# Three moves in a written order: a mask table, the second expert's pick, the first expert's rows

## The chip, the cores and the metric

The kernel runs on 1 core of one Trainium2 chip. The core has five engines, each with a queue of its own that it works off in order: TensorE (PE in the profile; its weight loads are PEld), VectorE (DVE), ScalarE (ACT), GpSimd (POOL) and SyncE (SP). SP issues most transfers, POOL and ACT issue some. The metric is device time of one execution in microseconds (us); 475.47 us is the median of three runs of the kernel before.

## The reference

Three layers are computed in float32: windowed attention with a few global positions, a routed expert layer in which a token may keep the expert of the token before it, and a gated two-matrix layer.

```python
scores = scale * q @ k.T - slopes * dist          # B=2, H=8, S=768, D=64; slopes = 2**-(h+1)
keep = (pos[None, :] < 8) | ((rel >= 0) & (rel < 96))
a = softmax(where(keep, scores, -1e9));  x = a @ v            # x: 2 x 768 x 512

logits = x @ w_gate                                # 8 experts
local_gate = sigmoid(x @ w_local)
e[s] = argmax(logits[s]) if s == 0 or local_gate[s] < 0.5 else e[s - 1]
out[s] = softmax(logits[s])[e[s]] * (relu(x[s] @ w1[e[s]]) @ w2[e[s]])   # 512 -> 1024 -> 512

xk = mu_k * x + (1 - mu_k) * x_prev;  xr = mu_r * x + (1 - mu_r) * x_prev
out = sigmoid(xr @ w_r) * (relu(xk @ w_k)**2 @ w_v)
```

## The kernel before

**Attention.** The 2 x 768 tokens are twelve tiles of 128. Each tile takes two steps of the main loop (`i`, 24 in all, `t, g = divmod(i, 2)`), one for each four heads. A step has six parts: scores on TensorE into PSUM (`emit_S`); masks and minima on VectorE (`emit_min`, L922: score plus a mask table `tb`, and the row's minimum); exponentials on ScalarE (`emit_exp`, L934, with row sums); transposes of the weights (`emit_pT`, L941 and L943, into banks PT); their eviction to SBUF, one half by VectorE and one by ScalarE (`emit_ev`, L952 and L950, tiles `pt`); and output products (`emit_pv`, L966, into a bank O), which come one or two steps later. `emit_xT` (L971) evicts the finished tile `xT`, `turn_x` (L188) turns it to rows, and `route_x` (L193) writes rows `X`.

**Mask tables.** The eight tables of 128 x 232 (`tables`, L604) are made by VectorE in the first steps. They wait in a list `tq`; `NTAB` says how many are taken at the end of a step.

**Routing.** It runs in pairs of tiles, spread over the attention's steps: logits on TensorE (`route_lgt`, L215, bank R), maxima and candidates `ab` on VectorE (`route_max`, `route_max2`), `ab` turned into rows (`route_rows`, L267; ScalarE evicts half of it as `br`, L270), a scan over the tokens (`route_scan`, L278, `er`), the one-hot `OH` (`route_oh`, L291), and sums of it on TensorE (`route_sum`, L303 and L307) that give every row its place in the expert's region. GpSimd scatters the rows to HBM (`scatter`, L311).

**First experts early.** The expert with most rows so far is picked from the first tiles (`early_pick` rank 0), and the kernel begins its work before the routing is over. A second pick (rank 3, matmul L375, `bonus` L373, `early_index` cast L380) names the next expert; `values_load` (L983) reads the cast's result on SP. The first expert's first 128 rows are read back from HBM into `xe` (`early_x`, L990), turned and split into a high and a low part: `early_split` transposes (L693), evicts the high part on ScalarE (`exexh`, L695) and subtracts on VectorE (`exexl`, L697). All matmuls of the experts are three products of such parts (`mm3`, L683 to L685, with weights `whi`, L667, and `wlo`, L672). The remaining work of the first expert is fed in by a generator (`fill`, advanced by `F_`) between the last steps of the routing.

**What sets the order.** The order on every engine is the order in which this code is written (`tc.manual_schedule`). In the main loop there are named points (`Rs`, `Ra`, `Dq`, `Dm`, ...): `at(i, point, f)` puts routing work at a point of step `i`, and `do(i, point)` runs it there. The last step (`i = 23`) is written out behind the loop. A tile's PSUM bank is taken from a pool by its tag (S, T, O, PT, R); bank R exists once, so every user of it waits for the reader of the one before.

Of the kernel before, what the change touches and what calls it, by code (L numbers as in the profile page):

```python
# [47 lines left out]
XW = (3, 4, 5, 7)  # L48
NIN = 4
NI = 2 * NTT  # L50
NTAB = (5, 4)
X1_AT = (5, 7)
WNEXT = (1, 1, 1, 0, 0, 1, 2, 1, 2, 1, 2, 0) + (0,) * 4
EARLY_AT = (7, 9, 9, 10, 10, 11, 11, 11, 12, 12, 12, 13, 13, 13, 15, 15, 15, 15)
# [564 lines left out]
def build(ctx, tc, ins, out):  # L619
    n = Net(ctx, tc, ins, out)  # L620
# [352 lines left out]
    def early_split(a):  # L973
        ex = [ap.tile([P, KD, P], F32R, tag=tg, bufs=2, name=f"ex{tg}{a}") for tg in ("exh", "exl")]
        yield from split_steps(xe[a], *ex, 0, n.bank("T", 1) if a else n.bank("S", 2))
        xe[a] = ex
# [4 lines left out]
    def early_start(rank, r):  # L981
        fi = n.early_index(rp, rank)
        wsrc[r] = nc.values_load(fi[:, 0:1], engines=(SP,), min_val=0, max_val=E - 1)  # L983
# [23 lines left out]
    def at(i, point, *fs):  # L1007
        plan.setdefault((i, point), []).extend(fs)
# [12 lines left out]
    for g in groups:  # L1021
        i = 2 * g[-1] + 3
        lgg, mx, mx2, rows, scan, tn, oh, sm_, ps_, acc = (lambda f=f, g=g: f(ap2, g) for f in (
            lambda _, g: n.route_lgt(ap2, g, xTs), n.route_max, n.route_max2, n.route_rows, n.route_scan, n.route_turn, n.route_oh, n.route_sum,
            lambda _, g: pos(g), n.route_acc))
        if g[-1] == NTT - 1:
            tail = mx, mx2, rows, scan, tn, oh, sm_, ps_
            continue
        at(i, "Rb", lgg)
        at(i + 1, "E0" if g[-1] < NTT - 3 else "Ra", lambda g=g: n.route_lge(ap2, g))  # L1030
        at(i + 1, "Rb", lambda g=g: n.route_lgb(ap2, g))
        at(i + 1, "Db", mx)
        if g[-1] < NTT - 3:
            at(i + 1, "Db", mx2)
        if g[-1] == NTT - 3:
            tail8 = mx2, rows, scan, tn, oh, sm_, ps_, acc
            continue
        at(i + 2, "Ra", rows)
        at(i + 2, "Dm", scan)
        at(i + 3, "Rt", tn, oh)  # L1040
        at(i + 3, "Rb", sm_)
        if g[-1] in (5, 7):
            e = g[-1] == 7

            def count(g=g, e=e):
                nm = "cnte" if e else "cnt6"
                setattr(n, nm, n.counted(rp, g, nm))
                n.route_mm(ap2, g)
                n.order_a(ap2, "fg"[e], getattr(n, nm), n.fvec if e else None)

            at(i + 3, "Rb", count)
            at(i + 3, "Db", lambda g=g: pos(g, False), acc)
            at(i + 3, "Rc", n.order_k)
            at(i + 3, "Dc", lambda e=e: n.order_c(ap2, "fg"[e], rp))
            at(i + 4, "Ra" if e else "Rs", lambda e=e: n.early_pick(rp, 3 * e))
            at(i + 4, "Dm" if e else "Dq", lambda e=e: early_start(3 * e, e))
        else:
            at(i + 3, "Db", ps_, acc)

    with tc.manual_schedule():  # L1060
# [99 lines left out]
        for i in range(NI - 1):  # L1160
            t, g = divmod(i, 2)
            late = g == 1 and i > 1
            ahead = [] if i and not g else [u for u in (i + 1, i + 2) if u < NI and u // 2 == (i + 1) // 2]

            def scores():
                for u in ahead:
                    emit_S(u)
                for u in ahead:
                    if u // 2 % NT < NT - 1:
                        emit_kglob(u)  # L1170
                if i == 0:
                    emit_kglob(0)

            def next_kq(*turned):
                emit_kT(t + 1, *turned[0:1])
                if t + 2 < NTT:
                    load("k", t + 2)
                emit_qT(t + 1, *turned[1:2])
                if t + 2 < NTT:
                    load("q", t + 2)  # L1180

            turned = []
            if late:
                scores()
                emit_xT(t - 1)
                emit_exp(i, 0)
                emit_exp(i, 1)
                do(i, "Rs")
                emit_pT(i - 1, 0)
                emit_pT(i - 1, 1)  # L1190
                if i < NI - 2:
                    emit_min(i + 1)
                do(i, "Dq")
                emit_ev(i - 1, 0)
                emit_ev(i - 1, 1, True)
                do(i, "Ra")
                n.turn_x(xTs[t - 1], t - 1, "O" if i < NI - 3 else "S")
                do(i, "Dm")
            else:
                if i > 2 and t + 1 < NTT and not g:  # L1200
                    turned = [turn4(kn.pop(t + 1)), turn4(qn.pop(t + 1))]
                do(i, "Rt")
                if 0 < i:
                    emit_pT(i - 1, 0)
                    emit_pT(i - 1, 1)
                do(i, "Ra")
                emit_exp(i, 0)
                do(i, "E0")
                if turned:
                    next_kq(*turned)  # L1210
                if 0 < i:
                    emit_ev(i - 1, 0)
                    emit_ev(i - 1, 1, True)
                if i == 2:
                    turned = [None]
                    next_kq()
                emit_exp(i, 1)
                if i and g == 0:
                    n.route_ri(t - 1, stat[t - 1][1])
                do(i, "Dm")  # L1220
            bg_early()
            if i == 1:
                n.routing_consts()
            if not late:
                scores()
            if scq:
                scatter(scq.pop(0))
            if g == 0 and t + 1 < NTT and not turned:
                next_kq()
            do(i, "Rb")  # L1230
            bg_early()
            if i < NI - 2 and not late:
                emit_min(i + 1)
            if late:
                if t - 1 in XW[::2]:
                    n.xw = wp.tile([P, 2 * D], F32, tag="whi", bufs=9, name=f"xw{t - 1}")
                n.route_x(ap, X, t - 1)
            do(i, "Db")
            for u in (i - 2, i - 1) if i and not g else ():
                emit_pv(u, 0)  # L1240
                emit_pv(u, 1)
            do(i, "Rc")
            do(i, "Dc")
            if g == 0 and 0 < t and (t + 1) % NT and t + 1 < NTT:
                load_vp(t + 1)
            for _ in scq[:2]:
                scatter(scq.pop(0))
            if g == 1 and t + 2 < NTT:
                load("v", t + 2)
            if 0 < i <= E // 2:  # L1250
                for e in (2 * i - 2, 2 * i - 1):
                    nc.scalar.dma_start(out=n.xs[e * REG:e * REG + PRE, :], in_=n.warm)
            if tq:
                for _ in range(NTAB[i]):
                    if tq:
                        tq.pop(0)()
                if not tq:
                    tstack.close()
                    n.counters(ap)
                    dp = astack.enter_context(tc.tile_pool(name="dp", bufs=1, reuse_waits="tile"))  # L1260
                    dwa = dp.tile([P, 1024], F32, name="dwa")
            if i == 2:
                n.routing_fill()
            if i == 3:
                n.gate_rest()
                n.mix_load()
            if i == 4:
                n.mix_rest()
                n.limits(n.const)
            if 0 in wsrc and early is None:  # L1270
                early = True
                ld_q = list(range(4))
                hi_q = [None] * 3 + [(c, s_) for c in range(NIN) for s_ in range(2)]
                bg_early()
            if i in (4, 11, 17):
                dec_load(PIECES[(4, 11, 17).index(i)], dwa)
            if i in (7, 12):
                dgen = dec(PIECES[i // 12], word_tile)
            if i in (7, 8, 9, 12, 13, 15):
                next(dgen, None)  # L1280
            if i == NI - 2:
                dec_load(PIECES[3], qzz)
# [11 lines left out]
        i = NI - 1  # L1294
# [6 lines left out]
        mx2()  # L1301
        emit_min(i)
        emit_ev(i - 1, 1, True)
        first_rows = early_split(0)
        next(first_rows)
        n.turn_x(xTs[a], a)
        rows()
        scan()
        n.route_x(ap, X, a)
        for _ in first_rows:  # L1310
            pass
        emit_exp(i, 0)
        emit_exp(i, 1)
        for _ in range(2):
            bg_early(0)
        emit_pv(i - 1, 0)
        emit_pv(i - 1, 1)
        tn()
        oh()
        while hi_q or lo_q:  # L1320
# [730 lines left out]
```

## Time and profile before

| | |
|---|---|
| median of 3 runs | 475.47 us (474.75 to 476.24) |
| the profiled execution | 478.9 us, span 477.1 us |
| TensorE busy | 461.9 us (97%) |
| VectorE busy | 345.2 us (72%) |
| ScalarE busy | 267.1 us (56%) |
| GpSimd busy | 115.9 us (24%) |
| read from and written to HBM | 73.49 MB and 12.71 MB |

The span goes from the first instruction to the last; the execution's own time is 1.8 us longer. Attention with the routing fills about the first 106 us, the experts follow, and the last layer closes. All times below count from the span's start. Matmuls are pipelined: a row's duration overlaps that of the next one, so distances between starts tell more than durations.

### The profile page before, as it was taken

The page shows a single profiled execution, that of the slowest core. Times are in us where ns is not written, and L with a number is a line of the kernel's source. Part 1 is how long each engine was busy: PE and PEld are TensorE (multiplying, and loading weights), DVE is VectorE, ACT ScalarE, POOL GpSimd, SP SyncE. Part 2 cuts the span into 40 slices and gives each one's busy share as a digit, 9 for nine tenths or more (in the row PEclk, how much of TensorE's full clock was granted, in tenths as well). Part 3 has the DMA queues.
Part 4 walks back from the last instruction along what each step waited for, and adds up shares of the span by engine and source line. Part 5 has one row for each costly group of instructions (what it writes and reads, how often), then busy time and mean ns, then how long its engine had stood idle before and what let it go on. Part 6 is the DMA issues. An engine that isn't in the chain of part 4 may idle for free. (4 is left out here: it accounts for less than half of the span.)

```text
span 477.1 us, 9261 instructions
## 1 busy us (share of the span) xinstructions
PE 461.9 (97%) x3210; PEld 399.4 (84%) x3210; DVE 345.2 (72%) x911; ACT 267.1 (56%) x657; POOL 115.9 (24%) x204
## 2 busy tenths in 40 slices
PE   7999999989999999999999999999999999999994
PEld 5888888768788889879879887898989898898984
DVE  5878898986859867988897988897848767363301
ACT  3898888974437735577696686752424324152320
POOL 4212212202300000000010013061844819162220
PEclk9999999999999999999999999999999999999999
DMA  7997586967576887799699733004738450200001
GB/s 178 252 225 175 147 212 204 281 208 235 182 246 217 301 288 242 237 332 311 210 357 405 249 117 111 23 2 128 281 100 279 138 185 38 88 1 23 23 3 49
DMA packets 76491, 86.90 MB, mean 182 GB/s; under 512 B 50676, under 2 KB 50932, under 8 KB 76436
## 3 DMA queue, kind: packets, MB, share of 16 engines
q1 hardware_dynamic: 68176, 63.01, 42.2%
q0 software_dynamic: 4944, 17.17, 11.1%
q10 hardware_dynamic: 3316, 6.03, 3.5%
q8 instruction: 28, 0.46, 0.4%
q14 instruction: 27, 0.22, 0.1%
HBM read 73.49 MB, written 12.71 MB: 181 GB/s over the span
## 5 line engine op out<-in xcount | busy, mean ns | idle before, releaser
L667 ACT ACTIVATE whi<-wraw 128x512 fp32r<-128x512 f32 x128 | 72.4, 623 | 6.9 <-ACT yo L786 2.2
L676 DVE TENSOR_TENSOR wlo<-wraw,whi 128x1024 fp32r<-128x1024 f32 x55 | 66.1, 1218 | 2.9 <-ACT whi L667 2.4
L1562 ACT ACTIVATE sq<-S 128x256 f32<-128x256 f32 x48 | 18.5, 385 | 72.9 <-PE S L685 72.5
L683 PE MATMUL S<-xkh,whi 128*128 128x256 f32 x192 | 54.3, 283 | 0.2 <-ACT whi L667 0.2
L685 PE MATMUL S<-xkh,wlo 128*128 128x256 f32 x192 | 53.3, 278 | 0.2 <-DVE wlo L672 0.2
L1572 POOL TENSOR_TENSOR kl<-sq,kh 128x256 fp32r<-128x256 f32 x40 | 36.6, 923 | 69.5 <-issue 36.6
L684 PE MATMUL S<-xkl,whi 128*128 128x256 f32 x192 | 53.2, 277 | 0.0
L1602 DVE TENSOR_TENSOR o<-O,sig 128x512 f32<-128x512 f32 (+1 forms) x13 | 8.4, 650 | 50.9 <-PE O L685 31.7
L684 PE MATMUL O<-wlo,kh 128*128 128x512 f32 (+1 forms) x104 | 39.1, 376 | 0.7 <-DVE wlo L672 0.7
L685 PE MATMUL O<-whi,kl 128*128 128x512 f32 (+1 forms) x104 | 39.1, 376 | 0.0
L683 PE MATMUL O<-whi,kh 128*128 128x512 f32 (+1 forms) x104 | 38.7, 373 | 0.0
L683 PEld LDWEIGHTS S<-xkh,whi 128*128 128x128 f32 x192 | 36.1, 188 | 0.7 <-ACT whi L667 0.4
L685 PEld LDWEIGHTS S<-xkh,wlo 128*128 128x128 f32 x192 | 36.1, 188 | 0.4 <-DVE wlo L672 0.4
L684 PEld LDWEIGHTS S<-xkl,whi 128*128 128x128 f32 x192 | 36.1, 188 | 0.2
L1563 DVE SCALAR_TENSOR_TENSOR sq<-S,sq 128x256 f32<-128x256 f32 x48 | 20.1, 421 | 15.8 <-ACT sq L1562 15.3
L1571 ACT ACTIVATE kh<-sq 128x256 fp32r<-128x256 f32 x48 | 19.7, 412 | 12.9 <-DVE sq L1563 12.9
L684 PEld LDWEIGHTS O<-wlo,kh 128*128 128x128 f32 x104 | 19.5, 188 | 4.9 <-DVE wlo L672 1.1
L683 PEld LDWEIGHTS O<-whi,kh 128*128 128x128 f32 x104 | 19.5, 188 | 3.7
L685 PEld LDWEIGHTS O<-whi,kl 128*128 128x128 f32 x104 | 19.6, 188 | 3.5
L311 POOL DMA_INDIRECT xs<-X,posi x8 | 9.6, 1197 | 44.0 <-DVE acc L333 18.6
L952 DVE COPY pt<-PT 128x512 f32<-128x512 f32 (+1 forms) x24 | 15.4, 641 | 5.9 <-PE PT L943 4.2
L966 PE MATMUL O<-pt,vn 128*64 128x128 f32 x192 | 18.7, 281 | 0.6 <-ACT pt L950 0.4
(488 smaller groups left out, 1424.0 us busy)
## 6 DMA issues: line engine op xcount, KB each, us to landing
wraw<-in_moe_w_dram SPq DMA_DIRECT2D x64, 512.0 KB
dwt<-in_moe_w_v_dram POOLq DMA_DIRECT2D x8, 512.0 KB, 4.2
z<-in_moe_w_k_dram SPq DMA_DIRECT2D x8, 512.0 KB
z<-in_moe_w_v_dram SPq DMA_DIRECT2D x8, 512.0 KB
ys<-yo ACTq DMA_DIRECT2D x13, 256.0 KB
vn<-in_v_dram SPq DMA_DIRECT2D x12, 256.0 KB
xn<-xs SPq DMA_DIRECT2D x12, 256.0 KB
dwt<-in_moe_w_k_dram POOLq DMA_DIRECT2D x6, 512.0 KB, 6.4
```

The lines of the kernel that those rows point to most:

```text
L311: self.nc.gpsimd.indirect_dma_start(self.xviews[t], bass.IndirectOffsetOnAxis(ap=self.posi[:, t:t + 1], axis=0), X[t], None)
L667: nc.scalar.activation(out=whl[r, c][0][:, sl], in_=raws[r, c][:, sl], func=ACTF.Copy)
L676: nc.vector.tensor_tensor(lo, raws.pop((r, c)), hi.bitcast(F32), op=ALU.subtract)
L683: nc.tensor.matmul(out_, lhsT=ah, rhs=bh, start=first, stop=False)
L684: nc.tensor.matmul(out_, lhsT=ah, rhs=bl, start=False, stop=False)
L685: nc.tensor.matmul(out_, lhsT=al, rhs=bh, start=False, stop=last)
L952: nc.vector.tensor_copy(d[:, 0:ps.shape[1]], ps)
L966: nc.tensor.matmul(Os[t][a * HD:(a + 1) * HD, p * P:(p + 1) * P], lhsT=src[:, h * HD:(h + 1) * HD], rhs=d[:, (2 * c + a) * P:(2 * c + a + ...
L1562: nc.scalar.activation(out=sq_, in_=ps[:, 0:TB], func=ACTF.Relu)
L1563: nc.vector.scalar_tensor_tensor(sq_, ps[:, 0:TB], 0.0, sq_, op0=ALU.max, op1=ALU.mult)
L1571: nc.scalar.activation(out=hh, in_=sq_, func=ACTF.Copy)
L1572: (nc.gpsimd if b else nc.vector).tensor_tensor(hl, sq_, hh.bitcast(F32), op=ALU.subtract)
```

## The change

Three pieces of work change their place; no operation is added or taken away. First, the list of mask tables is emptied between the two evictions of step 2, and `NTAB` takes fewer at the end of step 1. Second, the second pick moves to a new point `Rp` ahead of the minima of step 21, and its cast to `Dq`, behind the minima and ahead of the evictions. Third, in the last step its exponentials and the output products of the step before it come ahead of `early_split(0)`, which began right behind the evictions.

```diff
-NTAB = (5, 4)
+NTAB = (5, 2, 0)
...
-            at(i + 4, "Ra" if e else "Rs", lambda e=e: n.early_pick(rp, 3 * e))
-            at(i + 4, "Dm" if e else "Dq", lambda e=e: early_start(3 * e, e))
+            at(i + 4, "Rp" if e else "Rs", lambda e=e: n.early_pick(rp, 3 * e))
+            at(i + 4, "Dq", lambda e=e: early_start(3 * e, e))
...
                 emit_pT(i - 1, 0)
                 emit_pT(i - 1, 1)
+                do(i, "Rp")
                 if i < NI - 2:
                     emit_min(i + 1)
                 do(i, "Dq")
...
                     emit_ev(i - 1, 0)
+                    while i == 2 and tq:
+                        tq.pop(0)()
                     emit_ev(i - 1, 1, True)
...
-            if tq:
+            if tq or i == 2:
                 for _ in range(NTAB[i]):
...
         emit_ev(i - 1, 1, True)
-        first_rows = early_split(0)
-        next(first_rows)
         n.turn_x(xTs[a], a)
         rows()
         scan()
+        emit_exp(i, 0)
+        emit_exp(i, 1)
+        emit_pv(i - 1, 0)
+        emit_pv(i - 1, 1)
+        first_rows = early_split(0)
+        next(first_rows)
         n.route_x(ap, X, a)
         for _ in first_rows:
             pass
-        emit_exp(i, 0)
-        emit_exp(i, 1)
         for _ in range(2):
             bg_early(0)
-        emit_pv(i - 1, 0)
-        emit_pv(i - 1, 1)
         tn()
         oh()
```

On VectorE, at the mask tables, there stood (a `pt` is evicted from bank PT, `tb` is a mask table, `RI` the reciprocal of row sums):

```order
L922 ISA peexl,nm_309<-S_296,tb 128x232
L922 ISA nm_309 128x1
L604 SCALAR_TENSOR_TENSOR tb<-rel,mw 128x232 x3
L952 COPY pt_0_340<-PT_332 128x256
L198 TENSOR_SCALAR RI<-sm_208 128x8
```

and now there stands

```order
L922 ISA peexl,nm_309<-S_296,tb 128x232
L922 ISA nm_309 128x1
L604 SCALAR_TENSOR_TENSOR tb<-rel,mw 128x232 x2
L952 COPY pt_0_329<-PT_321 128x256
L604 SCALAR_TENSOR_TENSOR tb<-rel,mw 128x232
L198 TENSOR_SCALAR RI<-sm_208 128x8
```

One table, the eighth, has gone behind the eviction. On VectorE, at the second pick in step 21, there stood (`Rg` is the ranking, `fi` the index that SP reads, `R` the bank of the pick; four minima stand between the first two rows and the eviction):

```order
L364 TENSOR_SCALAR Rg<-iota_e,rkg 8x8
L922 ISA peexh,nm_1694<-S_1666,tb 128x232
...
L922 ISA peexl,nm_1694<-S_1667,tb 128x232
L922 ISA nm_1694 128x1
L952 COPY pt_0_1700<-PT_1684 128x512
L373 SCALAR_TENSOR_TENSOR bonus<-Rf,Rg 8x1
L380 CAST fi_1713<-R_1706 1x1
L672 TENSOR_TENSOR wlo_1_1605<-wraw_1_1458,whi_1_1604 128x512 x2
```

and now there stands

```order
L364 TENSOR_SCALAR Rg<-iota_e,rkg 8x8
L373 SCALAR_TENSOR_TENSOR bonus<-Rf,Rg 8x1
L922 ISA peexh,nm_1698<-S_1666,tb 128x232
...
L922 ISA peexl,nm_1698<-S_1667,tb 128x232
L922 ISA nm_1698 128x1
L380 CAST fi_1704<-R_1696 1x1
L952 COPY pt_0_1716<-PT_1684 128x512
L672 TENSOR_TENSOR wlo_1_1605<-wraw_1_1458,whi_1_1604 128x512 x2
```

`bonus` has gone ahead of the minima and the cast ahead of the eviction; on TensorE the pick keeps its place. On TensorE, in the last step, there stood (`xe` holds the first expert's rows, `xT` the finished tile, `R` receives the rows of `ab`, `O` the output products):

```order
L943 MATMUL PT_1810<-ident,peexl 128x128
L693 MATMUL S_1831<-ident,xe_1664 128x128 x4
L188 MATMUL PT_1837<-ident,xT_1815 128x128 x4
L267 MATMUL R_1842<-ident,ab_1781 1x128 x4
L966 MATMUL O_1862<-pt_0_1817,vn_1565 64x128 x2
...
L966 MATMUL O_1862<-pt_1_1827,vp 64x128 x2
L286 MATMUL R_1871<-ones_r,er_1849 128x8 x2
```

and now there stands

```order
L943 MATMUL PT_1810<-ident,peexl 128x128
L188 MATMUL PT_1829<-ident,xT_1815 128x128 x4
L267 MATMUL R_1834<-ident,ab_1781 1x128 x4
L966 MATMUL O_1847<-pt_0_1817,vn_1565 64x128 x2
...
L966 MATMUL O_1847<-pt_1_1827,vp 64x128 x2
L693 MATMUL S_1858<-ident,xe_1664 128x128 x4
L286 MATMUL R_1871<-ones_r,er_1841 128x8 x2
```

The four transposes of `xe` have gone behind the output products. On ScalarE, in the same step, there stood (the four rows L934 are the last step's exponentials):

```order
L950 ACTIVATE pt_1_1827<-PT_1810 128x512
L695 ACTIVATE exexh_1829<-S_1831 128x512
L270 ACTIVATE br_1847<-R_1842 1x256
L934 ACTIVATE zbig,sm_1695<-zbig,nm_1694 128x232
...
L934 ACTIVATE peb_108,sm_1695<-peb_108,nm_1694 128x232
L667 ACTIVATE whi_4_1893<-wraw_4_1624 128x512 x2
```

and now there stands

```order
L950 ACTIVATE pt_1_1827<-PT_1810 128x512
L270 ACTIVATE br_1839<-R_1834 1x256
L934 ACTIVATE zbig,sm_1699<-zbig,nm_1698 128x232
...
L934 ACTIVATE peb_108,sm_1699<-peb_108,nm_1698 128x232
L695 ACTIVATE exexh_1856<-S_1858 128x512
L667 ACTIVATE whi_4_1893<-wraw_4_1624 128x512 x2
```

The eviction `exexh` has gone behind `br` and the four exponentials. VectorE's order in the last step is what it was: `er`, X, `exexl`, `wlo`, `OH`. SP's and GpSimd's orders are unchanged.

## Rows read from the trace of the kernel before

**Rows 1.** The page's first part: busy time, share, instructions.
```profile
PE 461.9 (97%) x3210; PEld 399.4 (84%) x3210; DVE 345.2 (72%) x911; ACT 267.1 (56%) x657; POOL 115.9 (24%) x204
```

**Rows 2.** Timeline, TensorE, 84 to 112 us: start, duration, what, [wait before <-releaser].
```profile
94.19 0.65 PE L215 MATMUL R<-xT,wgb 128*32 128x128 f32 x16 [0.40 <-DVE pt L952]
...
100.52 0.66 PE L693 MATMUL S<-ident,xe 128*128 128x128 f32 x4 [1.52 <-DMA xe<-xs]
...
103.28 0.38 PE L286 MATMUL R<-ones_r,er 1*128 1x8 f32 x2 [0.21 <-DVE er L278]
...
105.75 0.28 PE L303 MATMUL R<-OH,tri 128*128 128x16 f32 x1 [0.21 <-DVE OH L291]
```

**Rows 3.** Timeline, TensorE, 18 to 20 us.
```profile
18.31 0.66 PE L966 MATMUL O<-pt,vn 128*64 128x128 f32 x8 [0.18 <-DVE pt L952]
...
19.85 0.46 PE L908 MATMUL O<-zbig,qz 64*128 64x232 f32 x1
```

**Rows 4.** Timeline, VectorE, 16 to 20 us.
```profile
16.61 1.31 DVE L604 SCALAR_TENSOR_TENSOR tb<-rel,mw 128x232 f32<-128x232 f32 x3
17.84 0.41 DVE L952 COPY pt<-PT 128x256 f32<-128x256 f32 x1
...
19.39 0.40 DVE L922 CUSTOM_DVE_ANT_0 peb<-O,tb 128x232 f32<-128x232 f32 x1
```

**Rows 5.** Timeline, VectorE, 93 to 96 us, around the cast.
```profile
93.33 0.67 DVE L952 COPY pt<-PT 128x512 f32<-128x512 f32 x1
93.94 0.14 DVE L373 SCALAR_TENSOR_TENSOR bonus<-Rf,Rg 8x1 f32<-8x1 f32 x1
94.00 0.14 DVE L380 CAST fi<-R 1x1 int32<-1x1 f32 x1
...
95.87 0.67 DVE L952 COPY pt<-PT 128x512 f32<-128x512 f32 x1
```

**Rows 6.** Timeline, TensorE, 101 to 103 us, the last step.
```profile
101.01 0.60 PE L188 MATMUL PT<-ident,xT 128*128 128x128 f32 x4
101.45 0.60 PE L267 MATMUL R<-ident,ab 128*1 128x128 f32 x4
101.98 0.44 PE L966 MATMUL O<-pt,vn 128*64 128x128 f32 x4
```

**Rows 7.** Timeline, ScalarE, 99 to 106 us.
```profile
99.10 0.60 ACT L950 ACTIVATE pt<-PT 128x512 f32<-128x512 f32 x1
101.21 0.60 ACT L695 ACTIVATE exexh<-S 128x512 fp32r<-128x512 f32 x1 [1.52 <-PE S L693]
102.09 0.37 ACT L270 ACTIVATE br<-R 1x256 f32<-1x256 f32 x1 [0.28 <-PE R L267]
102.37 0.47 ACT L934 ACTIVATE zbig<-zbig,nm 128x232 f32<-128x232 f32 x1
...
104.26 1.14 ACT L667 ACTIVATE whi<-wraw 128x512 fp32r<-128x512 f32 x2
```

**Rows 8.** Timeline, VectorE, 100 to 106 us.
```profile
100.10 0.16 DVE L257 SCALAR_TENSOR_TENSOR ab<-fr,fl 128x2 f32<-128x2 f32 x1
...
101.14 0.39 DVE L922 CUSTOM_DVE_ANT_0 peb<-O,tb 128x232 f32<-128x232 f32 x1
...
102.49 0.74 DVE L278 TENSOR_TENSOR_SCAN er<-R,er,br 1x256 fp32r<-1x256 f32 x1 [0.95 <-ACT br L270]
...
103.74 0.67 DVE L697 TENSOR_TENSOR exexl<-S,exexh 128x512 fp32r<-128x512 f32 x1
104.34 1.27 DVE L672 TENSOR_TENSOR wlo<-wraw,whi 128x512 fp32r<-128x512 f32 x2
105.54 0.15 DVE L291 TENSOR_TENSOR OH<-R,iota_e 128x16 fp32r<-128x16 f32 x1
```

**Rows 9.** Timeline, SP's queue, 96 to 102 us.
```profile
97.85 0.34 SPq L990 DMA_DIRECT2D xe<-xs  x1
```

**Rows 10.** Everything that touches tile xs, its last line: transfers in us.
```profile
DMA to landing us min/median/max: 2.8/4.5/5.1
```

## The prediction

> **What bounds the kernel now.** I read the profile from the coarse to the fine. TensorE is busy for 97% of the span [rows 1], so only its waits can give time back without less work. The second view is TensorE's own list in order of time, for the stretch from 84 to 112 us, where two of the three edits lie: it shows four waits [rows 2]. 0.40 us before the router's products at 94.19, 1.52 us for the first expert's rows at 100.52, 0.21 us for the scan `er` and 0.21 us for the one-hot `OH`. The third view is the same list around 18 us, for the mask tables: 0.18 us before the products at 18.31 [rows 3]. Were all the waits that the edits aim at to go and nothing to come late behind them, 0.18 + 0.40 + 1.52 = 2.10 us would be won, 0.44% of the span. That is the ceiling. The question is what is late next at each place.
>
> **Mask tables.** By `NTAB` (5, 2, 0 for 5, 4) two tables seem to move. The order shows one: the old loop made the three tables left of eight in front of the eviction, the new one makes two there, and only the eighth comes behind it. Three tables run from 16.61 to the eviction at 17.84, 0.41 us each [rows 4]. The eviction moves up by 0.41, and the products at 18.31 by their whole wait, 0.18. But the next tile's score on bank O starts at 19.85 [rows 3], 0.06 us after VectorE's minimum that frees the bank ends (19.39 + 0.40 = 19.79) [rows 4]. That minimum has the same instructions ahead of it as before, so it does not move, and TensorE gives the 0.18 back there. The ends are -0.18 and 0; I take 0. No DMA and nothing on GpSimd changes its turn.
>
> **Second pick.** The cast of the index now runs straight after the four minima, ahead of the eviction, and `bonus` ahead of the minima. The cast matters to TensorE because the router's products at 94.19 write the bank that the cast reads: the wait there is put down to the eviction, and it ends 0.05 us after the cast (94.00 + 0.14) [rows 2, 5]. Now the minima end up to 0.14 us later (`bonus` is 0.14 long), the cast starts at about 93.33 + 0.13 = 93.46 and ends at 93.60, and the products can start near 93.7: TensorE is 0.47 ahead. What is pushed back is the eviction, by 0.19 (93.33 to 93.52), and everything behind it on VectorE by 0.06 at most, since the same instructions are done by then. The next eviction at 95.87 is in that shadow. SyncE's load of the index does not profit: in its queue it stands behind the transfer of `xe`, which is issued only at 97.85 [rows 9], so no weight load moves. Alone the edit would run into the wait for `xe` and be worth 0; the ends are +0.13 (the minima late for nothing) and -0.47. I take 0 by itself, and 0.06 as the delay that it leaves on VectorE.
>
> **First expert's rows.** This is the large wait, and its chain has to be followed to its end. Before: the transposes of `xe` start at 100.52 [rows 2], the turn of `xT` at 101.01, the rows of `ab` at 101.45 [rows 6], ScalarE evicts `br` at 102.09 and starts four exponentials at 102.37 [rows 7], the scan `er` at 102.49, then `exexl` at 103.74, `wlo` at 104.34, `OH` at 105.54 [rows 8], and TensorE's sums at 105.75 [rows 2].
> After: the turn of `xT` waits for ScalarE's eviction of the bank, 99.10 + 0.60, some 0.3 us sooner by the second edit, so it starts at 99.5 to 99.8. The second half of the rows needs the last write of `ab`, 100.10 + 0.16 + 0.06 = 100.32 [rows 8]; it starts at 100.38 and its two transposes end at about 100.76 (four of them take 0.60, 0.11 apart [rows 6]). `br` starts at 100.80, 1.29 us earlier. The output products follow at 100.6 and take 1.09 (from 101.98 to 103.07, where the wait for `er` begins [rows 2, 6]), so `xe` is turned from 101.7 to 102.35 (0.66), without a wait: it had landed by 100.5.
> Then comes what is late next. On ScalarE `exexh` now stands behind the exponentials. `br` takes 0.28 to the next start, the four exponentials 104.26 - 102.37 = 1.89, so `exexh` starts at 100.80 + 0.28 + 1.89 = 102.97 and ends at 103.57 (0.60) [rows 7]. On VectorE `er` starts at 101.6, where the minima end (101.14 + 0.39 + 0.06), and the product X is done by 102.9; then VectorE waits for `exexh`. `exexl` starts at 103.63, 0.06 after it. Before it was 103.74. Behind it stand `wlo` and `OH` as before: `OH` at 105.43 for 105.54. TensorE has all its work up to the sums done early and waits about 1 us for `OH`. Of 1.52 us, 0.11 is left. The ends are -1.52 (if `OH` were not in the way) and +0.84 (below); I take -0.11, from the rows of the chain itself.
>
> **The sum.** 0 + 0 - 0.11 = -0.1 us on the profiled execution's 478.9 (span 477.1 and 1.8 around it): 478.8. It is 3.4 us above the median of the runs, 475.47; the difference is taken over: 475.4 us, and that is no change. Behind the sums the same view has no further wait of TensorE up to 112 us [rows 2], so I let what is won or lost at `OH` stand to the end.
>
> **Rivals.**
> A, everything is won: TensorE's 2.10 us, to 473.4. For it: the three waits are real and their successors on TensorE are ready. Against it: `OH` on VectorE behind `exexl` and `wlo`, 1.9 us of work after `exexh`.
> B, slower: `xe` lands sooner in an execution without the profiler, and then the old order has little to lose while the new one still holds `exexh` behind four exponentials. If `xe` is there by about 99.6, `br` of before also starts at 100.80, `er` follows the minima at 101.54 instead of 102.49, and `OH` comes 0.95 sooner; the new order stays, so it is 0.95 - 0.11 = 0.84 slower: 476.3. The point at which it turns is a landing 0.11 us before 100.52. For it: the scattered rows that `xe` waits for land after 2.8 to 5.1 us, median 4.5 [rows 10], so 1.7 us sooner is in reach. Against it: the transfer competes with weight loads.
> The trace has 2.67 us from the issue of `xe` at 97.85 to its first use [rows 2, 9]. The Trainium skill (DMA: Bandwidth & Descriptors, Latency and other measured facts) puts an access to HBM at 0.2 us on average and 2 us at high load. By that, as an estimate, `xe` could be there 1.8 us sooner, at 98.7, and the time would be that of B; by the row there is a wait, and the sum is mine.
> C, `xe` lands later, by the 0.6 us between median and longest [rows 10]: the old order pays all of it, the new one has over 1 us of cover: 475.47 - 0.7 = 474.8.
> D, the pick alone slows the stretch: VectorE's 0.13 us with no cover, 475.6, decided where the minima, not the exponentials, end last. It falls within the forecast.
>
> **How the numbers follow.** Forecast with D 0.53, A 0.16, B 0.20, C 0.11. A measurement of this kernel can tell some 0.3%, 1.4 us, from no change. Faster by more needs below 474.0: most of A (0.14) and an outer part of C (0.03): 0.17. Slower by more needs above 476.9: an outer part of B (0.07, `xe` early and the exponentials late too) and what the reading of one execution leaves out (0.04): 0.11. The rest is 0.72. The range goes from 473.9, which leaves out the better part of A, to 476.7, which takes in B and 0.4 beyond.
>
> **What would show it.** Right: no wait before the transposes of `xe`, which stand behind the output products; a wait of about 1 us before the sums (L303), released by `OH`; VectorE idle 0.7 us before `exexl`, released by `exexh`; the wait before the router's products at 94.19 gone; and TensorE waiting for VectorE before the O scores at 19.85. Wrong: the sums (L303) more than 0.5 us away from 0.1 before where they were, against the same instruction of another execution; or the index load on SyncE moved with the cast.

## The result, and the profile after

The changed kernel took 480.38 us (median of 4 runs, 479.39 to 480.46), the kernel before 475.86 beside it (4 runs): a ratio of 1.0094, interval 1.007 to 1.0117. It is 4.5 us slower, where no change was forecast and 476.7 was the end of the range. In a second comparison, with ten runs, the loss came again: 480.28 against 476.64, 1.0052 (1.0028 to 1.0075). Ratios in this document leave out four runs that took over 1.5% longer than the fastest of their kernel (one with the wait for the turn filled, two with `OH` first, one with the products in the wait); medians and counts have them in.

The page of the changed kernel: busy time by engine, and the granted clock in forty slices of 12 us.

```profile
PE 463.8 (97%) x3210; PEld 400.4 (84%) x3210; DVE 343.5 (72%) x911; ACT 266.4 (56%) x657; POOL 116.0 (24%) x204
...
PEclk9999999987999999999999999999999999999998
```

TensorE's 3210 matmuls are those of [rows 1], but they take 1.9 us more. The second line says where: the clock is down in the ninth and tenth slices. The chain that was predicted lies just ahead of that. TensorE after the change (start, duration, what, [wait before <-releaser]):

```profile
89.31 0.66 PE L188 MATMUL S<-ident,xT 128*128 128x128 f32 x4 [0.24 <-DVE nm L922]
...
95.56 0.66 PE L188 MATMUL PT<-ident,xT 128*128 128x128 f32 x4 [0.75 <-ACT pt L950]
...
97.75 0.66 PE L693 MATMUL S<-ident,xe 128*128 128x128 f32 x4
...
101.63 0.28 PE L303 MATMUL R<-OH,tri 128*128 128x16 f32 x1 [0.79 <-DVE OH L291]
```

These answer to [rows 2]. The wait for `xe` is gone, and 0.75 us ahead of the turn of `xT` in the last step (95.56) and 0.79 us ahead of the sums have come. The 0.40 us before the router's products are gone too, but 0.24 us for the last minimum stand one instruction sooner. VectorE after the change, the cast and then the last step:

```profile
89.50 0.14 DVE L380 CAST fi<-R 1x1 int32<-1x1 f32 x1
89.58 0.67 DVE L952 COPY pt<-PT 128x512 f32<-128x512 f32 x1
...
97.55 0.73 DVE L278 TENSOR_TENSOR_SCAN er<-R,er,br 1x256 fp32r<-1x256 f32 x1
...
99.60 0.69 DVE L697 TENSOR_TENSOR exexl<-S,exexh 128x512 fp32r<-128x512 f32 x1 [0.73 <-ACT exexh L695]
...
101.41 0.17 DVE L291 TENSOR_TENSOR OH<-R,iota_e 128x16 fp32r<-128x16 f32 x1
```

and ScalarE, with `br` and the eviction behind the exponentials:

```profile
96.83 0.37 ACT L270 ACTIVATE br<-R 1x256 f32<-1x256 f32 x1 [1.32 <-PE R L267]
...
99.00 0.57 ACT L695 ACTIVATE exexh<-S 128x512 fp32r<-128x512 f32 x1
```

These answer to [rows 5, 7, 8]. All stand some 4 us earlier than before, most of which is not the change's: this execution started faster (last section). A measure for it is TensorE's matmul of the second pick, whose place among TensorE's instructions the change leaves as it was. Before:

```profile
92.89 0.18 PE L375 MATMUL R<-Rg,iota_p 8*1 8x1 f32 x2
```

After, with the router's products behind it:

```profile
88.89 0.18 PE L375 MATMUL R<-Rg,iota_p 8*1 8x1 f32 x2
...
89.90 0.64 PE L215 MATMUL R<-xT,wgb 128*32 128x128 f32 x16
```

It is 4.00 us ahead. The cast is 3.96 us ahead of its predicted 93.46, `br` 3.97, `exexh` 3.97, `exexl` 4.03, `OH` 4.02. The chain is right to a tenth of a microsecond. Against [rows 2] the sums are 4.12 us ahead, so 0.12 of that is the change's.

Behind the sums that lead is lost. The windows of the kernel before (busy us of PE, PEld, DVE, ACT, POOL, then the granted clock, DMA share, GB/s):

```profile
98.00:104.00 6.00, 4.27 (x42) 3.48 (x43) 4.91 (x22) 4.20 (x13) 0.00 (x0) 1.00 0.78 244
104.00:114.50 10.50, 10.17 (x81) 8.03 (x80) 7.23 (x30) 3.44 (x8) 2.98 (x3) 1.00 0.47 150
114.50:130.00 15.50, 14.91 (x85) 11.70 (x84) 13.26 (x44) 7.87 (x14) 3.54 (x3) 1.00 0.66 230
```

and of the changed kernel:

```profile
98.00:104.00 6.00, 5.08 (x41) 3.51 (x41) 5.13 (x17) 3.09 (x10) 0.55 (x1) 1.00 0.59 224
104.00:114.50 10.50, 10.50 (x47) 8.74 (x44) 2.82 (x16) 1.56 (x3) 2.43 (x3) 0.51 0.75 240
114.50:130.00 15.50, 14.94 (x85) 11.67 (x84) 13.59 (x44) 7.87 (x15) 3.48 (x3) 1.00 0.41 139
```

From 104 to 114.5 us TensorE never waits, runs at 0.51 of its clock (1.2 GHz, the lower of its two levels), and gets through 47 matmuls, against 81 in the same window before. The two windows do not hold the same work, since this execution is 4 us ahead, so the measure is the length of equal rows (L207 are the router's products of the last tile, and the transposes of `hnk` close the stretch). Before:

```profile
108.68 1.07 PE L207 MATMUL R<-wgb,xT 128*128 128x18 f32 x8
...
111.18 0.63 PE L188 MATMUL PT<-ident,xT 128*128 128x128 f32 x4
...
114.18 0.60 PE L693 MATMUL PT<-ident,hnk 128*128 128x128 f32 x4
```

After:

```profile
104.88 1.89 PE L207 MATMUL R<-wgb,xT 128*128 128x18 f32 x8
...
109.59 1.09 PE L188 MATMUL PT<-ident,xT 128*128 128x128 f32 x4
...
114.84 0.60 PE L693 MATMUL PT<-ident,hnk 128*128 128x128 f32 x4
```

4.12 us ahead at the sums, 0.66 us behind at the turn of `hnk`: 4.78 us are lost in this stretch, and that is the loss. From the sums to that turn it takes 13.21 us, before 8.43.

### The profile page after: what moved, and what is told of

Its sections match the earlier page's. It is cut to its first block, busy times and chain, and to the rows that moved or that the text cites. A ratio compares the mean times of both kernels' runs of the same rounds, so it can differ in the third digit from the quotient of the medians.

```text
span 478.6 us, 9262 instructions
## 1 busy us (share of the span) xinstructions
PE 463.8 (97%) x3210; PEld 400.4 (84%) x3210; DVE 343.5 (72%) x911; ACT 266.4 (56%) x657; POOL 116.0 (24%) x204
## 4 chain that ended last, share of the span: by engine, by line
PE 34%; issue 9%; DVE 5%; ACT 2%; DMA 2%; POOL 0%; POOLq 0%; ACTq 0%; DVEq 0%
PE S L685 5%; PE S L683 5%; PE S L684 5%; PE O L684 4%; PE O L685 4%; PE O L683 4%; PE PT L685 2%; PE PT L684 2%; PE PT L683 2%; DMA dwt<-in_moe_w_v_dram 1%; DVE wlo L676 1%; DVE wlo L672 1%; ACT whi L667 1%; DMA yg<-ys,yposi 1%; PE T L1509 1%
## 5 line engine op out<-in xcount | busy, mean ns | idle before, releaser
L685 PE MATMUL PT<-whi,xrl 128*128 128x512 f32 x48 | 19.0, 395 | 0.0
```

What stands on the lines that cost most here:

```text
L685: nc.tensor.matmul(out_, lhsT=al, rhs=bh, start=False, stop=last)
```

## The experiments

Theory 1: the granted clock falls because of waits that the change gives TensorE. In form 1a it is the wait for `OH`, in form 1b the thin use earlier in the step. The rival: the fall has another cause, such as the other two edits, the execution or the chip. Each kernel ran 10 to 12 times beside the kernel before (the change 4 and 10 times). A run's mean clock tells whether a fall was in it: .995 to .999 without one, about .987 with ten microseconds at the lower level, .990 to .994 with fewer. In the table a run "with a fall" has .994 or less; one run of the kernel before and one with the products in the wait have just .994. The ratios are not quotients of the medians beside them.

| kernel | runs with a fall | median us | kernel before | ratio (interval) |
|---|---|---|---|---|
| before, beside the four groups of experiments | 3 of 109 (0 of 31, 0 of 34, 3 of 27, 0 of 17) | | 476.71; 475.98; 476.64; 476.04 | |
| change, both comparisons | 12 of 14 | 480.38; 480.28 | 475.86; 476.64 | 1.0094 (1.007 to 1.0117); 1.0052 (1.0028 to 1.0075) |
| rows alone | 6 of 10 | 480.08 | 476.71 | 1.0051 (1.0017 to 1.0084) |
| tables and pick | 1 of 10 | 478.07 | 476.71 | 1.0026 (1.0 to 1.0051) |
| pick alone | 1 of 10 | 478.26 | 476.71 | 1.0007 (0.998 to 1.0033) |
| tables alone | 1 of 10 | 476.47 | 476.71 | 1.0005 (0.9972 to 1.0037) |
| both waits filled | 0 of 12 | 476.83 | 475.98 | 1.0015 (0.9993 to 1.0036) |
| wait for `OH` filled | 0 of 12 | 476.52 | 475.98 | 1.0007 (0.9986 to 1.0027) |
| wait for the turn filled | 8 of 11 | 480.98 | 475.98 | 1.007 (1.0038 to 1.0102) |
| `OH` first | 4 of 12 | 479.04 | 475.98 | 1.0043 (1.0013 to 1.0073) |
| before, `OH` made late | 5 of 12 | 477.85 | 476.64 | 1.0028 (0.9995 to 1.0061) |
| products in the wait | 6 of 12 | 477.48 | 476.64 | 0.9999 (0.9971 to 1.0026) |
| no late wait | 0 of 12 | 475.25 | 476.04 | 0.9977 (0.9951 to 1.0002) |

**Which edit.** The three edits alone, and the first two together.

Rows alone: the last hunk of the diff (`early_split(0)` and the exponentials), with the other two edits undone.

> The first expert's rows moved alone (part three); mask tables and second pick as before. Theory 1 (the new order of the last step leaves TensorE too thinly used, and its clock falls from full to half at about 104 us for some 10 us): 479.5 to 481 us, ratio about 1.009, a half clock for about 10 us beginning near 104 to 108 us. Rival (the clock falls because the earlier parts bring the stretch forward or add a wait of their own, as 0.75 us before the turn of xT): 475 to 476, granted clock full from 98 to 116 us.

Six of ten runs had a fall, none of the 31 of the kernel before beside them. The profiled run fell; it has the two waits, 0.75 and 0.78 us, and its clock is at 0.50 from 108 to 116 us. The rows are enough.

Tables and pick together: the other hunks, with the last one undone.

> Mask table and second pick moved, the last step as before. Theory 1: 475 to 476 us, ratio 0.998 to 1.000, granted clock full from 98 to 116 us, and the wait for xe about 0.3 us longer than 1.5. Rival: about 480, with the fall of the clock near 104 us.

One fall, so falls in most runs need the rows. But the median is 2 us above what I expected: four of the ten runs took over 479 us with no fall in the clock. The interval starts at 1.0, so a cost of these two edits is neither shown nor excluded, and what made the four runs long stays open.

Pick alone: the hunks of `Rp` and `Dq` only.

> Second pick moved alone. Theory 1: 475.3 to 476.3 us, clock full; the 0.40 us before the router's products gone, and given back at xe. Rival: a fall of the clock, 479 to 480, if the pick alone makes it.

The ratio is 1 within its interval, though the median is 1.55 us above that of before. Its one fall is in the profiled run, and it comes elsewhere. TensorE there, and a window of its clock:

```profile
98.91 1.11 PE L693 MATMUL S<-ident,xe 128*128 128x128 f32 x4 [2.25 <-DMA xe<-xs]
```

```profile
100.00:104.00 4.00, 4.00 (x33) 3.06 (x31) 1.82 (x3) 2.83 (x11) 0.00 (x0) 0.71 0.81 314
```

The wait for `xe` is 2.25 us in this execution, and the turn of `xe` behind it takes 1.11 us instead of the 0.66 of [rows 2]. So the clock fell once with the old order of the last step too, here where `xe` came latest of the five profiled executions of that order.

Tables alone: the `NTAB` and `tq` hunks only.

> One mask table moved behind the eviction, nothing else. Theory 1: 475.3 to 476.3 us, clock full, the 0.18 us before the products of the first tile gone and given back at the next score on bank O. Rival: no statement other than a shift of all later work by at most 0.5 us.

No change, as predicted; one run with a fall (482.0 us, mean clock .986), of which there is no trace.

**Which wait.** The order of the change stays, and a matmul of zeros whose result nobody reads fills TensorE's waits. Both filled:

```
+        nc.tensor.matmul(n.bank("S", 2)[:, 0:384], lhsT=n.warm[:, 0:P], rhs=n.warm[:, 0:384], ...)
         n.turn_x(xTs[a], a)
...
+        nc.tensor.matmul(n.bank("T", 1)[:, 0:384], lhsT=n.warm[:, 0:P], rhs=n.warm[:, 0:384], ...)
         sm_()
```

> The changed kernel with two matmuls of zeros (128x384, never read) put into TensorE's two waits of the last attention step: one ahead of the turn of xT (0.75 us of wait before), one ahead of the sums behind OH (0.79 us). The order of everything else is the same. Theory 1 (the two waits let the granted clock fall): the clock stays full from 98 to 118 us in nearly every execution, mean clock .996 or more, and the time is that of the change without its loss, 480.4 - 4.8 = 475.6 on the chip of the first comparison, a little below the kernel before (-0.4, so ratio about 0.999). Rival (the fall comes from something else than TensorE's waits, the order or the execution): mean clock .987 in most runs and about 480.

No fall in twelve runs, and the order is still the change's, so it is not the order by itself. The median is 0.85 us above that of before, where I expected 0.4 below (0.9992); the interval holds the first and just leaves out the second. The filler only for `OH` (the second pair of lines):

> The changed kernel with only the second of the two fillers, a 128x384 matmul of zeros in the 0.79 us wait for OH. Theory 1a (the wait for OH, the nearer of the two to the fall, decides): no fall, about 475.6, ratio 0.999. Theory 1b (thin use before it decides, the wait for the turn of xT and the thin half us behind it): the fall still comes in more than half of the executions, 479 to 480.

No fall either, though the 0.75 us ahead of the turn stay. TensorE in this run:

```profile
96.38 0.66 PE L188 MATMUL PT<-ident,xT 128*128 128x128 f32 x4 [0.75 <-ACT pt L950]
...
101.50 0.81 PE L1331 MATMUL T<-warm 128*128 128x384 f32 x2
102.45 0.28 PE L303 MATMUL R<-OH,tri 128*128 128x16 f32 x1
...
105.38 1.07 PE L207 MATMUL R<-wgb,xT 128*128 128x18 f32 x8
```

The sums start no sooner than the wait would let them (12.76 us behind the second pick's matmul, 12.74 in the change), L207 takes 1.07 us as before the change, and the median is some 4 us below that of the change. The filler only ahead of the turn (the first pair):

> The changed kernel with only the first of the two fillers, a 128x384 matmul of zeros in the 0.75 us wait ahead of the turn of xT. Theory 1a (the wait for OH decides): the fall still comes in more than half of the executions, 479 to 480. Theory 1b (the earlier wait decides): no fall, about 475.6, ratio 0.999.

8 of 11 fell. In the profile of one that fell:

```profile
95.29 0.81 PE L1307 MATMUL S<-warm 128*128 128x384 f32 x2
96.20 0.66 PE L188 MATMUL PT<-ident,xT 128*128 128x128 f32 x4
...
102.28 0.28 PE L303 MATMUL R<-OH,tri 128*128 128x16 f32 x1 [0.78 <-DVE OH L291]
...
106.08 1.90 PE L207 MATMUL R<-wgb,xT 128*128 128x18 f32 x8
```

One wait is gone, the wait for `OH` is there, and L207 is at half rate. That decides for 1a against 1b.

**The wait without the change.** The kernel before, in its own order, with one more VectorE instruction ahead of `OH`:

```
         tn()
+        nc.vector.tensor_tensor(n.warm, n.warm, n.warm, op=ALU.add)
         oh()
```

> The kernel before, with none of the three edits, and one more VectorE instruction (128x512, zeros added to zeros, never read) ahead of OH: some 0.64 us by the rows of wlo (1.28 us for two of that size). TensorE's wait before the sums becomes 0.21 + 0.64 = 0.85 us, about what the change made it. Theory 1a (a wait of TensorE at this place lets the granted clock fall): mean clock .987 in a third to two thirds of the executions, where the kernel before had none in 65, and 476.0 + 0.6 + 4.8 = 481.4 in those; median 477 to 481. Rival (the new order of the change is needed, the wait alone is not enough): no fall, 476.6, ratio 1.001.

Five of twelve runs fell, all to a mean of .986 or .987. The kernel before had 3 falls in 27 runs beside them (3 in 109 in all), none below .992. TensorE in a run that fell:

```profile
96.45 0.66 PE L693 MATMUL S<-ident,xe 128*128 128x128 f32 x4 [0.98 <-DMA xe<-xs]
...
102.28 0.28 PE L303 MATMUL R<-OH,tri 128*128 128x16 f32 x1 [0.81 <-DVE OH L291]
```

and its windows:

```profile
100.00:102.00 2.00, 1.47 (x9) 0.82 (x7) 2.00 (x4) 1.79 (x5) 0.00 (x0) 1.00 0.13 51
102.00:104.00 2.00, 1.61 (x12) 1.11 (x13) 1.86 (x11) 0.00 (x0) 0.00 (x0) 1.00 0.00 0
104.00:106.00 2.00, 1.98 (x20) 1.70 (x20) 1.83 (x8) 0.00 (x0) 1.59 (x2) 0.56 0.02 4
106.00:108.00 2.00, 2.00 (x11) 1.94 (x10) 0.00 (x0) 0.60 (x1) 1.39 (x2) 0.50 0.66 254
```

The wait for `OH` rose from 0.21 us [rows 2] to 0.81, and about 2 us behind it the clock is at half. With none of the three edits in the kernel, this rules out the rival that the other edits or the new order are needed. It is the count of falls that says so: the interval of the ratio, 0.9995 to 1.0061, still takes in 1.

**Taking the wait away by order.** The change with `OH` moved on VectorE ahead of `exexl`, into the time in which VectorE waits for `exexh`:

```
         n.route_x(ap, X, a)
+        tn()
+        oh()
         for _ in first_rows:
             pass
         for _ in range(2):
             bg_early(0)
-        tn()
-        oh()
```

> The changed kernel with OH moved on VectorE ahead of exexl and wlo, into the 0.73 us in which VectorE waits for exexh. No filler: the wait for OH is taken away by the order. Both theories of the local chain: OH at about 98.9 instead of 101.4, no wait before the sums, 0.79 us won there at full clock. Theory 1a: the clock stays full as well, so 480.4 - 4.8 - 0.8 = 474.8, ratio 0.997 against the kernel before. Theory 1b (the earlier wait decides): the clock still falls, about 479.5.

Missed: 4 of 12 fell. The wait for `OH` is gone, but one has come at TensorE's next product that needs VectorE (the profiled run, which did not fall):

```profile
104.41 0.18 PE L387 MATMUL R<-Rf,cnt 8*1 8x1 f32 x2 [1.05 <-DVE cnt L337]
```

That this wait took the clock down in the four others is not shown, since none of them has a trace. Next, on top of that edit, the last tile's output products moved into the new wait:

```
         F_(1)
+        emit_pv(i, 0)
+        emit_pv(i, 1)
         early_row()
         scatter(scq.pop(0))
-        emit_pv(i, 0)
-        emit_pv(i, 1)
```

> The changed kernel with OH ahead of exexl (as in the run where OH comes first) and, on TensorE, the products for the first expert's row (L387, which there waited 1.05 us for the count) moved behind the last tile's 16 output products. At most a short wait for the eviction of the last minima is left of the two behind OH. Theory 1a: no fall of the clock in 9 of 10 executions or more, about 1 us won against the kernel before, 475.0 to 475.5 where the kernel before has 476, ratio .998. Theory 1b (thin use earlier in the step): the clock falls in a third of the executions or more, 478 or above.

Missed again: 6 of 12 fell, all of them for less than ten microseconds, and the ratio is 1. L207 now had to wait for VectorE to read its bank.

```profile
106.08 1.07 PE L207 MATMUL R<-wgb,xT 128*128 128x18 f32 x8 [0.79 <-DVE erow L393]
```

Here the clock fell behind that wait, at about 108 us, in the second group of L207. The changed kernel itself ran beside this one and the kernel with `OH` made late:

> The changed kernel itself, on the same chip as the two others, for the count of executions in which the clock falls. Theory 1a: more than half, as with the rows' part alone (6 of 10) and with the filler ahead of the turn only (8 of 11); median 479.5 to 481, ratio 1.007. Rival (the loss was of the first chip): median about 476 and no fall.

8 of 10 fell. With the rows alone and the filled turn the fall has now come in three comparisons on three chips, so it is not a matter of one. Last, the products-in-the-wait version with the first expert's row in another bank, so that L207 need not wait:

```
         c9 = self.cnt9
-        ep = self.bank("R", 1)
+        ep = self.bank("T", 1)
```

> As the run with the output products in the wait, and the first expert's row (L387) written to bank T instead of R, so that the router's products (L207), which there waited 0.79 us for VectorE to read R, need not wait. Of TensorE's waits from 96 to 116 us only the 0.75 us ahead of the turn of xT is left. Theory 1a: the clock stays full (mean .996 or more) in 11 of 12 executions or more, and about 1 us is won against the kernel before: ratio .997 to .999, 475.3 to 476 where the kernel before has 476.6. Theory 1b (thin use earlier in the step decides): falls in a third of the executions or more, ratio above 1.002.

No fall in twelve runs, and the lowest ratio of all. TensorE's only wait left in the last step, and the clock:

```profile
97.44 0.66 PE L188 MATMUL PT<-ident,xT 128*128 128x128 f32 x4 [0.75 <-ACT pt L950]
```

```profile
98.00:106.00 8.00, 8.00 (x77) 5.86 (x76) 7.14 (x29) 4.86 (x14) 0.77 (x1) 1.00 0.54 197
106.00:114.00 8.00, 7.91 (x48) 6.48 (x47) 5.40 (x20) 3.19 (x7) 2.21 (x3) 1.00 0.71 213
```

With this wait removed as well the falls are gone, though the thin use earlier in the step is still there: form 1b expected them in a third of the runs. Against the changed kernel the gain is plain: 475.25, not 480.3. Against the one before, 0.9977 has an interval that just takes in 1, so a gain of about 1 us is the best estimate and not a proof.

## Why the prediction was wrong

**Right: the chain.** Every link of the third edit came within 0.1 us of its predicted place. VectorE waits 0.73 us for `exexh` (0.7 predicted), TensorE 0.79 us for `OH` (1 predicted), and the wait for `xe` is gone. The turn of `xT` waits for ScalarE's eviction and starts 3.94 us ahead of the predicted 99.5. From the second pick's matmul to the sums it takes 12.74 us, before 12.86: 0.12 less, where 0.11 was forecast.

The second edit alone stands at 1.0007 (0.998 to 1.0033), forecast as 0. Its end of -0.47 was too far out, since TensorE waited only 0.40 there: from L375 to the router's products it takes 1.01 us now and took 1.30, a gain of 0.29. In rival B the minima end at 101.54, while the chain above it has them end at 101.59; that makes B 0.05 smaller.

The table's gain is given back at the O scores, which start 0.06 us behind the end of the minimum that frees the bank, as in [rows 3, 4]. TensorE:

```profile
16.49 0.46 PE L908 MATMUL O<-zbig,qz 64*128 64x232 f32 x1
```

VectorE:

```profile
16.03 0.40 DVE L922 CUSTOM_DVE_ANT_0 peb<-O,tb 128x232 f32<-128x232 f32 x1
```

**Right as far as shown: the sum at full clock.** With the wait for `OH` filled the change stands at 1.0007 (0.9986 to 1.0027): no change, as the sum of -0.1 us had it. The interval is 1 us to either side, so it cannot tell -0.1 from a small loss.

**Wrong: "I let what is won or lost at `OH` stand to the end."** This step is the one that failed, and it costs the prediction 4.5 us between the medians. It took a microsecond of TensorE's waiting for a microsecond, whatever its place. TensorE's 1.52 us for `xe` became 0.75 and 0.79 us elsewhere, the same sum, and behind the second of these the clock fell in 12 of 14 runs. It is followed by the sums, some 0.65 us of matmuls on 1 to 16 columns: between 100.84 and 102.28 us TensorE had next to nothing to stream, and from 104 us it ran at half rate for ten microseconds. All durations behind `OH` were read from a trace at full clock. The term that was missing is 4.8 us (4.78 in the stretch above), times the share of runs in which it falls due. The sign that the prediction named for being wrong, the sums in another place, did not come, measured from the second pick's matmul: the loss lies behind them.

**The rivals.** None named the clock. B had the right sign and the wrong cause: `xe` did land sooner in some runs (waits of 0.95 to 2.25 us in the five profiled executions of the old order), but even a full B would be 0.8 us. Its mechanism does show at full clock: with the tables alone `xe` kept TensorE waiting 0.95 us, and the old order reached the sums 12.29 us behind the second pick's matmul, 0.45 less than the new one. A failed for the reason given against it, `OH` behind `exexl` and `wlo`.

What stays open: which runs fall. The same order falls in 8 of 10 runs here and in all of 4 there, and in the profiled executions the waits differ by hundredths of a microsecond. Why the change's rows alone fall in 6 of 10 and the whole in 12 of 14 is not settled by so few runs either. Nor is it settled whether the second edit is free at full clock. From the turn of `hnk` to the end the four profiled executions without it took 362.9 to 363.2 us, the ten with it 363.0 to 364.8; five of the ten have a wait of 0.74 us for VectorE's `sq` in the last layer, which none of the four has. It may be chance; no run tests it.

## What to carry to other kernels

When an edit moves a wait of TensorE rather than removing it, list TensorE's waits after the edit together with what it does just behind each. A wait of 0.8 us ahead of tiny matmuls cost ten microseconds at half clock here, 4.8 us of time, and the mean granted clock of each run told at once whether it did. To test that reason, fill the wait with a dummy matmul and leave the order alone. When you then take the wait away by order, look for the next instruction that needs the same slow engine: twice here a wait came at another place, and falls of the clock came with it.

## What the runs showed of the hardware

The clock fell after waits that are short. In [rows 2] a wait of 1.52 us left it full; 0.79 and 0.81 us ahead of the sums took it down in most runs (12 of 14, with the change) or nearly half of them (5 of 12, with `OH` made late). A wait of 1.05 us ahead of L387 left it full in the one run of that kernel that has a trace. So length alone does not decide. The Trainium skill (TensorE: Matmul & The Clock Gate, A second HAM failure mode: psum-queue depth-cycling) tells of a kernel whose frequent short pauses between groups of matmuls were enough to throttle it. The runs agree that short pauses can do it, and here a single one was enough; a clock that goes back and forth, as in that kernel, no trace here shows.

The start of an execution varies by some 3 us, whatever the kernel. The first scores in the kernel before:

```profile
7.45 1.23 PE L908 MATMUL S<-zbig,qz 64*128 64x128 f32 x8 [0.47 <-ACT qz L884]
```

and in the changed kernel, whose start has the same instructions:

```profile
6.68 0.72 PE L908 MATMUL S<-zbig,qz 64*128 64x128 f32 x8 [0.53 <-ACT qz L884]
```

By the O scores at 19.85 us [rows 3], which came at 16.49 after the change, the difference is 3.36 us. In the second profile of the changed kernel they came at 19.48. Over all 14 profiled executions they came at 16.4 to 17.4 us in ten and at 19.5 to 19.9 in four. This fits the 3.4 us by which the profiled execution before stood above its median, and the profiled run with both waits filled: 479.82 us at a mean clock of .996, its O scores at 19.47. It is not all of the spread: from the O scores to the second pick's matmul the 14 differ by another 1.7 us (72.40 to 74.12).

The profile's clock row says 1.00 in both starts; only the durations show it. Equal rows in the kernel before, some 5 us apart:

```profile
11.35 1.11 PE L865 MATMUL S<-ident,kn 128*128 128x128 f32 x4
...
16.50 0.60 PE L865 MATMUL S<-ident,kn 128*128 128x128 f32 x4
```

Four 128x128 transposes took 1.09 and 1.11 us above where the clock row was at half, and 0.60 at full. By that the slow start ran at half rate, and a run's mean clock does not tell of it.
